# An attention and token-MLP kernel on one core: a fixed order on all engines, hand-numbered PSUM banks, another way for the state and a guarded path with max

## The chip, the cores and the metric

The kernel runs on one core of a Trainium2 chip. The metric is the device time of one execution in microseconds (us), the median of several runs. The core has five engines with queues of their own: TensorE (PE, with its weight loads shown apart as PEld), VectorE (DVE), ScalarE (ACT), GpSimd (POOL) and SyncE (SP). SBUF is the working memory; PSUM, eight banks of 2 KB in each of 128 partitions, takes what TensorE computes, and VectorE and ScalarE copy it out ("evacuate" it).

## What is computed

Cross attention between a sequence `x` (8 batches, 8 heads, 512 tokens, 64 numbers) and a `state` of 32 rows per head, in both directions, and then a token-mixing MLP over the joined result. Cut to what matters:

```python
# x (8, 8, 512, 64), state (8, 8, 32, 64), all float32
scores = scale * x @ state.T;   scores -= scores.max(-1)
a = exp(scores);  a /= a.sum(-1) + 1e-9;     xread = a @ state
scores2 = scale * state @ x.T;  scores2 -= scores2.max(-1)
a2 = exp(scores2); a2 /= a2.sum(-1) + 1e-9;  sread = a2 @ x
y = concat([xread, sread], axis=2)           # heads joined: (8, 544, 512)
wq = y @ w_q;  wk = y @ w_k                  # (8, 544, 64)
mixed = (wq @ wk.T) * scale2 @ y             # (8, 544, 512)
out = maximum(mixed, 0) @ w_out              # (8, 544, 512)
```

## The kernel before

Each batch is one unit of work, and a batch is cut into two halves `u` of its sequence. The steps of a batch are short functions that are called by the names in one list, `ORDER` (line 16). A token such as `pt0.3.t` is the step `pt`, half 0, batch 3, engine `t` (TensorE; `v`, `a`, `p` are VectorE, ScalarE, GpSimd). The list fixes the order of TensorE alone (`manual_schedule`, line 63); the framework orders the other engines from the order of the list and its own rules.

The steps of batch `b`: `ix` (line 141) loads x as bfloat16 through a casting transfer that GpSimd issues; batch 0 comes as four float32 quarters `x_f0` (line 108) and is cast by `xc`. `xT` (line 217) transposes x on TensorE, `xTe` evacuates, `pt` (line 232) computes the scores, `exp` takes their exponential into `E`, without subtracting a maximum. `rs`, `rinv` and `A` (lines 266 to 288) sum and normalise by row; `at`, `ate` (lines 289, 299) transpose `A`. `srd`, `sums` (lines 303, 318) compute the other direction from the same `E`, `srn`, `sbd`, `srT` (lines 330 to 365) normalise it, place it as a block diagonal and transpose it. `wq`, `wk`, `g`, `v` (lines 366 to 462) are the small products of the MLP, `mix` (line 464) with its `relu` the mixed tokens, `fin` (line 509) the product with `w_o`, in pairs of 128 tokens, `oe`, `oc` (lines 521, 527) the copy to `ost` and the transfer to memory. `mixs` and `fs` do the same for the 32 state tokens, four batches at a time.

The state is loaded twice: batch 0 first (line 107), batches 1 to 7 later (line 111), in rows of 256 bytes. `stc` casts it, `stt` (line 173) transposes it, `ste`, `stf` evacuate it into `stT`. The block-diagonal copy `stbd` (128 rows of 4 blocks of 64 columns, zero outside the diagonal), which `v` needs, is filled by four scattering transfers out of `st_bf` (line 166). In `v_mm` all 128 rows take part in each matmul, most of them zeros:

```python
nc.tensor.matmul(out=ps, lhsT=L[b]["wk"][:, NC : NC + 2, :], rhs=L[b]["sbd"], start=True, stop=False)
for r in range(2):
    nc.tensor.matmul(out=ps[:, r, :, :], lhsT=L[b]["g"][:, r, :, :],
                     rhs=stbd[:, b, r, :, :], start=False, stop=(r == 1))
```

PSUM is cut into two pools: `psA` with two buffers of two banks (for `mix`, `fin`, `sw`) and `psB` with four buffers of one bank (all else); a step takes the next free buffer. The output copies of one bank, `ost1`, are used six times (the two `fse` and the four `oc`), and their pool `work` has four buffers (line 79).

Of the kernel before, what the change touches and what calls it, by code (L numbers as in the profile page):

```python
# [8 lines left out]
FP = mybir.dt.float32  # L9
BF = mybir.dt.bfloat16  # L10
# [11 lines left out]
sums.1.t xTe0.2.a A1.0.p pt1.2.t srn.1.v sw.3.t rs1.1.v exp1.2.a sbd.1.p srT.1.t at1.0.t pt0.2.t
rinv.1.v srTe.1.a xT0.3.t rs1.2.v exp0.2.a xT1.3.t A.1.p ate.0.a xTe1.3.v srd.2.t sums.2.t xTe0.3.v
pt1.3.t swe.1.a wq.0.t srn.2.v wks.0.t exp1.3.a rs0.2.v sw.2.t sbd.2.p wqe.0.a srT.2.t wk.0.t
rinv.2.v pt0.3.t srTe.2.a xT1.5.t wke.0.v exp0.3.a A.2.p xT1.4.t swe.3.v g.0.t xTe1.5.a srd.3.t
xTe1.4.v sums.3.t ge.0.a rs0.3.v pt1.5.t pt1.4.t exp1.5.a at.2.t srn.3.v exp1.4.a v.0.t ate.2.v
sbd.3.p srT.3.t swe.2.a at.1.t srTe.3.v rs1.4.v wq.2.t ve.0.a wks.2.t wqe.2.v wk.2.t mix1.0.t
# [24 lines left out]
def kernel(  # L52
# [10 lines left out]
    ctx.enter_context(tc.manual_schedule(engines={mybir.EngineType.PE}))  # L63
# [10 lines left out]
    HN = NP * NS  # L74
    scale = 1.0 / float(D) ** 0.5
# [18 lines left out]
    mask = const.tile([128, NP], BF, name="mask")  # L94
# [3 lines left out]
    rmix = const.tile([128, B, KC, 2, SH], BF, name="rmix")  # L98
# [42 lines left out]
    def load_x(n, b, e):  # L141
        if n == "iwo":
            nc.gpsimd.dma_start(out=w_o, in_=moe_w_out.rearrange("(k p) e -> p k e", p=128))
        else:
            b = int(n[2:])
            nc.gpsimd.dma_start(out=x_bf[b], in_=xsrc(b, 0, H))  # L146

    def x_cast(n, b, e):
        g = int(n[2:])
        o, i = x_bf[0][:, 2 * g : 2 * g + 2], x_f0[:, 2 * g : 2 * g + 2]  # L150
        if e == "p":
            nc.gpsimd.tensor_copy(out=o, in_=i)  # L152
# [9 lines left out]
    def st_cast(n, g, e):
        b0, b1 = (0, 1) if g == 0 else (1, B)
        copy(e, st_bf[:, b0:b1], st_f[:, b0:b1])
        if g == 1:
            for q in range(NP):
                rows = slice(NS * q, NS * q + NS)
                nc.sync.dma_start(
# [419 lines left out]
```

## Time and profile before

| | |
|---|---|
| time, median of three runs | 100.2 us (99.65, 100.2, 100.47) |
| span of the profiled execution, first to last instruction | 98.7 us |
| TensorE busy | 80.1 us in 1288 matmuls |
| ScalarE, VectorE, GpSimd busy | 56.9, 53.3, 35.0 us |
| read from and written to memory | 10.22, 8.91 MB |
| mean granted clock of TensorE | 0.944 of full speed |

The profile gives the span of its execution and no time of its own beside it; the 1.5 us between 98.7 and the median are what lies around the span. Busy time is the time in which an engine runs at least one instruction. Matmuls are pipelined: a group's busy time counts overlap once, the mean of one instruction does not. [...]

### The profile page before, as it was taken

To read this page: it belongs to the slowest core of one execution; us is meant where nothing else is said; L and a number is where in the kernel's file an instruction comes from. 1 tells how busy PE (TensorE), PEld (TensorE's weight loads), DVE (VectorE), ACT (ScalarE), POOL (GpSimd) and SP (SyncE) were. 2 spreads that over 40 slices of the span, in tenths; PEclk is the share of its full clock that TensorE was granted. 3 is DMA by queue.
4 is the path that set the end of the run, shared out by engine and by line. 5 is a ranking of instruction groups with operands and counts; after the bars stand their busy time and mean duration, and the time that the engine had idled before them with its cause. 6 is when DMAs were issued, how large, how long until landed. Compare 5 with 4: busy or idle time off the path is not lost.

```text
span 98.7 us, 2953 instructions
## 1 busy us (share of the span) xinstructions
PE 80.1 (81%) x1288; PEld 53.0 (54%) x1288; DVE 53.3 (54%) x107; ACT 56.9 (58%) x84; POOL 35.0 (35%) x42
## 2 busy tenths in 40 slices
PE   0137699654999999999999979999999999999200
PEld 0025588544889885584655736488646554344000
DVE  5443288870857891899148454555866760423200
ACT  2501958956078588184798776465964733855100
POOL 7289009999084910003800740570035200000000
PEclk9999999996559999999999999999999999999965
DMA  1999999999999200270324650283003255293980
GB/s 45 318 274 147 178 184 216 214 213 201 196 197 166 33 0 0 110 299 23 123 91 176 267 208 11 46 334 145 5 7 130 83 213 206 103 345 54 350 321 10
DMA packets 17044, 15.39 MB, mean 156 GB/s; under 512 B 5768, under 2 KB 14472, under 8 KB 17032
## 3 DMA queue, kind: packets, MB, share of 16 engines
q1 hardware_dynamic: 8392, 9.96, 31.8%
q0 software_dynamic: 7808, 4.19, 31.0%
q10 hardware_dynamic: 832, 1.05, 3.0%
q8 instruction: 10, 0.16, 0.7%
q14 instruction: 2, 0.02, 0.1%
HBM read 10.22 MB, written 8.91 MB: 194 GB/s over the span
## 4 chain that ended last, share of the span: by engine, by line
PE 60%; DMA 26%; POOL 3%; DVE 3%; ACT 2%; issue 1%; SPq 0%; ACTq 0%
PE fin_ps L505 22%; DMA x_bf<-in_x_dram 15%; DMA out_dram<-ost 6%; PE xT_ps L221 5%; PE mix_ps L471 4%; DMA x_f<-in_x_dram 4%; PE at_ps L295 3%; PE pt_ps L237 3%; PE wq_ps L371 3%; PE wk_ps L409 3%; PE srd_ps L308 2%; PE wk_ps L397 2%; PE fins_ps L505 2%; PE g_ps L425 2%; POOL x_bf L146 2%; PE v_ps L440 2%
## 5 line engine op out<-in xcount | busy, mean ns | idle before, releaser
L505 PE MATMUL fin_ps<-w_o,rmix 128*128 128x512 bf16 x128 | 29.9, 379 | 0.0
L282 POOL TENSOR_TENSOR A<-E,rinv 128x1024 bf16<-128x1024 bf16 (+1 forms) x8 | 14.4, 1804 | 21.4 <-DVE rinv L276 11.9
L505 PEld LDWEIGHTS <-rmix 128*128 128x128 bf16 x128 | 11.7, 98 | 12.7 <-issue 0.6
L221 PE MATMUL xT_ps<-ident,x_bf 128*128 128x128 bf16 x128 | 11.9, 255 | 4.1 <-POOL x_bf L152 1.8
L131 ACT COPY ost<-fin_ps 128x1024 f32<-128x1024 f32 (+1 forms) x10 | 9.3, 927 | 10.1 <-PE fin_ps L505 6.1
L137 ACT ACTIVATE rmix<-mix_ps 128x1024 bf16<-128x1024 f32 x12 | 12.2, 1025 | 4.0 <-PE mix_ps L471 4.0
L133 DVE COPY ost<-fin_ps 128x1024 f32<-128x1024 f32 (+1 forms) x8 | 8.7, 1090 | 10.1 <-PE fin_ps L505 10.1
L345 POOL TENSOR_TENSOR sbd<-srn,mask 128x256 bf16<-128x256 bf16 x16 | 9.5, 616 | 12.7 <-DVE srn L335 11.9
L268 DVE TENSOR_REDUCE rsum<-E 128x16 f32<-128x512 bf16 x16 | 10.7, 680 | 5.8 <-ACT E L253 5.7
L221 PEld LDWEIGHTS <-x_bf 128*128 128x128 bf16 x128 | 9.7, 116 | 5.4 <-POOL x_bf L152 2.1
L253 ACT ACTIVATE E<-pt_ps 128x512 bf16<-128x512 f32 x16 | 9.4, 604 | 4.3 <-PE pt_ps L237 3.8
L131 ACT COPY xT<-xT_ps 128x1024 bf16<-128x1024 bf16 x10 | 10.1, 1032 | 1.1 <-PE xT_ps L221 1.1
L237 PE MATMUL pt_ps<-stT,xT 128*128 128x64 bf16 x128 | 6.8, 205 | 0.8 <-ACT xT L131 0.8
L146 POOL DMA_DIRECT2D x_bf<-in_x_dram x7 | 6.8, 975 | 0.0
L237 PEld LDWEIGHTS <-xT 128*128 128x128 bf16 x128 | 5.5, 105 | 2.2 <-ACT xT L131 1.4
L133 DVE COPY xT<-xT_ps 128x1024 bf16<-128x1024 bf16 x6 | 4.1, 688 | 3.7 <-PE xT_ps L221 3.7
L179 PE MATMUL stT_ps<-ident,st_bf 128*64 128x128 bf16 x32 | 2.3, 314 | 4.5 <-DVE st_bf L133 4.5
L471 PE MATMUL mix_ps<-wq,V 64*128 64x256 bf16 x64 | 5.8, 272 | 0.1
L295 PE MATMUL at_ps<-ident,A 128*128 128x128 bf16 x64 | 5.1, 219 | 0.9 <-POOL A L282 0.9
L457 ACT ACTIVATE V<-v_ps 128x512 bf16<-128x512 f32 x6 | 3.6, 598 | 3.4 <-PE v_ps L444 3.2
L139 DVE TENSOR_SCALAR rmix<-mix_ps 128x1024 bf16<-128x1024 f32 x4 | 4.9, 1220 | 0.8 <-PE mix_ps L471 0.8
L295 PEld LDWEIGHTS <-A 128*128 128x128 bf16 x64 | 3.9, 98 | 1.5 <-POOL A L282 1.0
(71 smaller groups left out, 110.4 us busy)
## 6 DMA issues: line engine op xcount, KB each, us to landing
out_dram<-ost SPq DMA_DIRECT2D x14, 512.0 KB, 3.0
x_bf<-in_x_dram POOLq DMA_DIRECT2D x7, 512.0 KB, 12.3
out_dram<-ost SPq DMA_DIRECT2D x4, 256.0 KB, 4.7
x_f<-in_x_dram ACTq DMA_DIRECT2D x2, 256.0 KB, 3.6
x_f<-in_x_dram SPq DMA_DIRECT2D x2, 256.0 KB, 4.0
w_o<-in_moe_w_out_dram POOLq DMA_DIRECT2D x1, 512.0 KB, 12.8
out_dram<-ost ACTq DMA_DIRECT2D x2, 256.0 KB, 4.1
st_f<-in_state_dram SPq DMA_DIRECT2D x1, 448.0 KB, 6.4
```

Of the source, the lines that this page charges most:

```text
L131: nc.scalar.copy(out=out, in_=in_)
L133: nc.vector.tensor_copy(out=out, in_=in_)
L137: nc.scalar.activation(out=out, in_=in_, func=AF.Relu)
L221: nc.tensor.transpose(out=ps[:, h, :], in_=x_bf[b][:, h, 128 * u : 128 * u + 128], identity=ident)
L237: nc.tensor.matmul(out=ps[:, :, r, NS * q : NS * q + NS], lhsT=L[b][f"xTe{u}"][:, h, :], rhs=stT[:, b, h, :, :], start=(h == 0), stop=(h = ...
L253: nc.scalar.activation(out=L[b]["E"][:, 2 * u : 2 * u + 2].rearrange("p c r q n -> p c r (q n)"), in_=L[b][f"pt{u}"], func=AF.Exp, scale=f ...
L268: nc.vector.reduce_sum(out=L[b]["rsum"][:, w], in_=L[b]["E"].rearrange("p c r q n -> p (c r q) n")[:, w], axis=AX.X,)
L282: eng.tensor_tensor(out=L[b]["A"].rearrange("p c r q n -> p (c r q) n")[:, w], in0=L[b]["E"].rearrange("p c r q n -> p (c r q) n")[:, w], ...
L295: nc.tensor.transpose(out=L[b]["at"][:, r, c, :], in_=L[b]["A"][:, c, r, :, :], identity=ident)
L345: nc.gpsimd.tensor_tensor(out=L[b]["sbd"][:, r], in0=L[b]["srn"][:, r : r + 1, :].to_broadcast((128, NP, D)), in1=mask[:, :, None].to_broa ...
L471: nc.tensor.matmul(out=ps[:, h, kk, :], lhsT=L[b]["V"][rows, 128 * k : 128 * k + 128], rhs=L[b]["wq"][rows, 0:SH], start=True, stop=True,)
L505: nc.tensor.matmul(out=ps, lhsT=lhs(k), rhs=w_o[:, k, :], start=(k == 0), stop=(k == KC - 1))
```

## The change

- All engines follow the list now, not TensorE alone. A token has five parts: step, index, batch, engine, PSUM bank. The output transfers are tokens of their own (`d`, `dc`, `ds`), on SP.
- PSUM is one tile of eight banks, and each step is told its bank.
- The state is loaded once, as 128 rows of 4 KB (`st_c`), cast in halves, and transposed in 32 transposes. The block diagonal comes from `stT` by 64 small transposes (`sp`) and two products with a mask for each half of the batches (`stbd`); it has two blocks for each half of 64 rows in place of four for 128, and `v` works in two halves of 64 rows that write different banks.
- x0 and x1 come as float32 in plain quarter loads and are cast by engines. GpSimd's casting loads of x2 to x7 are spread over the list, the one of `w_o` comes after batch 0's `A`.
- Four groups of dummy matmuls (`dm`, 23, 17, 8 and 7 of 128 columns) stand at the start of TensorE's order.
- `A` and the reciprocals always go in halves.
- Output copies have a pool of their own with six buffers.
- The sums are kept in `chk`. At the end `ok` tests that all lie between 2^-60 and 2^60, `okm` and `oke` count them, every engine reads the count, and if it falls short a second program, `with_max`, computes all batches again with the maximum subtracted.

The core of the diff:

```diff
 ORDER = """
...
+xc.0.2.a.0 xc.0.0.p.0 xc.0.3.p.0 xc.0.1.v.0 ix.0.2.p.0 dm.128.23.t.7 xp.1.0.t.0 xp.0.0.t.1
+dm.128.17.t.7 xp.0.2.t.1 stc.0.1.p.0 xp.1.2.t.0 xp.1.3.t.0 xp.0.1.t.1 stc.0.0.v.0 xp.1.1.t.0
+xTe.1.0.a.0 xp.0.3.t.1 dm.128.8.t.7 stt.0.0.t.2 xc.1.2.p.0 dm.128.7.t.7 stt.0.1.t.2 xc.1.0.v.0
+xTe.0.0.v.0 ste.0.0.a.0 xq.1.0.t.0 ste.0.1.a.0 xc.1.1.v.0 stf.1.0.v.0 xq.1.2.t.0 xc.1.3.p.0
+xq.0.0.t.1 xq.1.1.t.0 wc.0.0.p.0 pt.0.0.t.4 xq.1.3.t.0 xq.0.2.t.1 xq.0.3.t.1 pt.1.0.t.5
+stf.1.1.a.0 ste.0.2.v.0 xq.0.1.t.1 xTe.1.1.v.0 xTe.0.1.v.0 exp.0.0.a.0 exp.1.0.a.0 sp.0.0.t.6
+stf.1.2.a.0 srd.0.0.t.7 pt.0.1.t.0 pt.1.1.t.1 rs.1.0.v.0 sums.0.0.t.7 sw.0.3.t.4 rs.0.0.v.0
+exp.1.1.a.0 rv.0.0.v.0 rs.1.1.v.0 swe.0.3.a.0 sp.0.1.t.6 rv.1.0.v.0 exp.0.1.a.0 sw.0.0.t.2
+A.0.0.p.0 srn.0.0.v.0 sw.0.1.t.4 rv.1.1.v.0 A.1.0.p.0 srd.0.1.t.0 rs.0.1.v.0 ix.0.3.p.0
...
+fin.3.2.t.0 at.0.3.t.5 d.0.1.s.0 exp.0.4.a.0 exp.1.4.a.0 xT.0.5.t.4 ix.0.6.p.0 xTe.1.5.v.0
+oe.1.1.a.0 at.1.3.t.5 pt.1.5.t.6 rs.0.4.v.0 srT.0.3.t.7 rs.1.4.v.0 sbd.0.3.v.0 xTe.0.5.a.0
+fin.0.2.t.2 exp.1.5.a.0 rv.0.4.v.0 ate.0.3.v.0 srTe.0.3.v.0 pt.0.5.t.4 wks.0.3.t.5 rs.1.5.v.0
+wq.0.3.t.6 exp.0.5.a.0 A.0.4.p.0 srd.0.4.t.7 srd.0.5.t.4 rv.1.4.v.0 oe.1.2.v.0 sums.0.4.t.7
+wqe.0.3.a.0 wk.0.3.t.5 wke.0.3.a.0 A.1.4.p.0 fin.1.2.t.2 sums.0.5.t.4 srn.0.4.v.0 d.1.1.s.0
+at.1.4.t.5 rs.0.5.v.0 oe.0.2.a.0 ix.0.7.p.0 srT.0.4.t.0 g.0.3.t.1 srn.0.5.v.0 xT.0.6.t.6
...
+mse.0.7.v.0 d.1.4.s.0 fs.0.7.t.6 fin.0.6.t.2 fin.1.6.t.2 mxe.0.7.v.0 fin.2.7.1.7 fse.0.7.v.0
+fin.3.7.1.6 fin.1.7.1.4 fin.0.7.1.5 oe.0.4.a.0 d.0.4.s.0 oe.0.6.a.0 oc.2.7.v.0 ds.0.7.s.0
+oc.1.7.v.0 okm.0.0.t.7 oc.3.7.a.0 d.0.6.s.0 dc.3.7.s.0 oc.0.7.a.0 dc.2.7.s.0 dc.1.7.s.0 dc.0.7.s.0
+oke.0.0.v.0
...
-    ctx.enter_context(tc.manual_schedule(engines={mybir.EngineType.PE}))
+    ctx.enter_context(tc.manual_schedule())
...
-    psA = ctx.enter_context(tc.tile_pool(name="psA", bufs=2, space=bass.MemoryType.PSUM))
-    psB = ctx.enter_context(tc.tile_pool(name="psB", bufs=4, space=bass.MemoryType.PSUM))
+    ostp = ctx.enter_context(tc.tile_pool(name="ostp", bufs=6))
+    gen = ctx.enter_context(tc.tile_pool(name="gen", bufs=1))
+    psum = ctx.enter_context(tc.tile_pool(name="psum", bufs=1, space=bass.MemoryType.PSUM))
...
+    banks = psum.tile([128, 8, 512], FP, name="banks")
+    def one(k):
+        return banks[:, k, :]
+    def two(k):
+        return banks[:, k : k + 2, :]
...
-    nc.sync.dma_start(out=st_f[:, 0], in_=st_src[:, 0:2])
+    st_cs = state.rearrange("b h (g j) d -> (b h g) j d", j=16)
     for g in range(4):
-        eng = nc.sync if g % 2 == 0 else nc.scalar
-        eng.dma_start(out=x_f0[:, 2 * g : 2 * g + 2], in_=xsrc(0, 2 * g, 2 * g + 2))
-    nc.sync.dma_start(out=st_f[:, 1:B], in_=st_src[:, 2 : 2 * B])
+        eng = nc.sync if g % 2 else nc.scalar
+        eng.dma_start(out=x_f[0][:, 2 * g : 2 * g + 2], in_=xsrc(0, 2 * g, 2 * g + 2))
+    nc.sync.dma_start(out=st_c, in_=st_cs)
+    for g in range(4):
+        nc.sync.dma_start(out=x_f[1][:, 2 * g : 2 * g + 2], in_=xsrc(1, 2 * g, 2 * g + 2))
...
+    def dummy(i, b, e, k):
+        for _ in range(b):
+            nc.tensor.matmul(out=one(k)[:, 0:i], lhsT=fill[:, 0:128], rhs=fill[:, 0:i], start=True, stop=True)
...
+    def st_sp(i, g, e, k):
...
+        for b in range(4 * g, 4 * g + 4):
+            for r in range(2):
+                for q in range(NP):
+                    nc.tensor.transpose(
+                        out=G["sp"][NS * q : NS * q + NS, b, r, :],
+                        in_=stT[0:64, b, NP * r + q, 0, :],
+                        identity=ident[0:64, 0:64],
+                    )
+    def st_bd(i, g, e, k):
+        for q in range(2):
+            out = stbd[:, 4 * g : 4 * g + 4, :, q, :]
+            in_ = G["sp"][:, 4 * g : 4 * g + 4]
+            if e == "a":
+                nc.scalar.activation(out=out, in_=in_, func=AF.Copy, scale=mask[:, q : q + 1])
+            else:
+                nc.vector.tensor_scalar(
+                    out=out, in0=in_, scalar1=mask[:, q : q + 1], scalar2=None, op0=ALU.mult
+                )
...
+    def v_mm(i, b, e, k):
+        ps = two(k)[:, :, 0 : 4 * D].rearrange("p m (r t) -> p m r t", r=2)
+        for m in range(2):
+            rows = slice(64 * m, 64 * m + 64)
+            nc.tensor.matmul(
+                out=ps[:, m],
+                lhsT=L[b]["wk"][rows, NC : NC + 2, :],
+                rhs=L[b]["sbd"][rows],
+                start=True,
+                stop=False,
+            )
         for r in range(2):
+            for m in range(2):
+                rows = slice(64 * m, 64 * m + 64)
+                nc.tensor.matmul(
+                    out=ps[:, m, r, :],
+                    lhsT=L[b]["g"][rows, r, :, :],
+                    rhs=stbd[rows, b, r, :, :],
+                    start=False,
+                    stop=(r == 1),
+                )
...
+    def ok_v(i, b, e, k):
+        nc.vector.tensor_scalar(out=okay, in0=chk, scalar1=1.0 / LIM, scalar2=None, op0=ALU.is_ge)
+        nc.vector.scalar_tensor_tensor(
+            out=okay_bf, in0=chk, scalar=LIM, in1=okay, op0=ALU.is_le, op1=ALU.mult
+        )
+    def ok_mm(i, b, e, k):
+        G["ok"] = one(k)[0:1, 0 : B * (NR + 2)]
+        nc.tensor.matmul(
+            out=G["ok"], lhsT=ones, rhs=okay_bf.rearrange("p b j -> p (b j)"), start=True, stop=True
+        )
+    def ok_ev(i, b, e, k):
+        nc.vector.reduce_sum(out=n_ok, in_=G["ok"], axis=AX.X)
+        nc.vector.tensor_copy(out=n_ok_i, in_=n_ok)
...
+    good = nc.values_load(n_ok_i[0:1, 0:1])
+    with tc.If(good < 128 * B * (NR + 2), preferred_fallthrough_block=False):
+        ident_f = gen.tile([128, 128], FP, name="ident_f")
+        nc.vector.tensor_copy(out=ident_f, in_=ident)
+        for b in range(B):
+            with_max(b)
```

## Rows read from the trace of the kernel before

**Rows 1.** The page, part 1: busy time, share of span, instructions.

```profile
PE 80.1 (81%) x1288; PEld 53.0 (54%) x1288; DVE 53.3 (54%) x107; ACT 56.9 (58%) x84; POOL 35.0 (35%) x42
```

**Rows 2.** Busy time by stretch: from:to, length, each engine, clock, DMA share, GB/s.

```profile
12.56:16.00 3.44, 3.44 (x98) 3.14 (x96) 2.76 (x6) 2.11 (x3) 0.97 (x3) 1.00 1.45 196
16.00:23.69 7.69, 4.39 (x140) 3.41 (x123) 5.13 (x13) 6.32 (x10) 7.67 (x10) 0.94 1.63 213
23.69:29.40 5.71, 5.71 (x117) 4.89 (x118) 3.38 (x8) 1.81 (x5) 2.96 (x3) 0.50 1.45 195
29.40:91.98 62.58, 61.73 (x909) 37.94 (x906) 37.23 (x68) 41.00 (x60) 16.44 (x17) 1.00 0.38 129
91.98:98.70 6.72, 0.01 (x1) 0.00 (x0) 0.00 (x0) 0.58 (x1) 0.00 (x0) 0.68 0.58 221
...
12.56:23.69 11.13, 7.83 (x212) 6.55 (x211) 7.89 (x18) 8.43 (x13) 8.64 (x12) 0.96 1.58 208
```

**Rows 3.** The same view for line 221, x's transposes (PE, PEld, clock).

```profile
12.90:15.00 2.10, 1.90 (x16) 1.68 (x16) 1.00 1.46 192
...
23.60:25.70 2.10, 1.89 (x16) 1.63 (x16) 0.50 1.44 192
29.40:30.60 1.20, 1.14 (x16) 0.98 (x16) 0.92 1.46 207
```

**Rows 4.** Timeline of the start: start, length, instruction, idle time before it.

```profile
11.03 0.61 PE L237 MATMUL pt_ps<-stT,xT 128*128 128x64 bf16 x8 [0.78 <-ACT xT L131]
...
15.93 2.62 POOL L146 DMA_DIRECT2D x_bf<-in_x_dram  x3
...
20.64 1.06 POOL L282 TENSOR_TENSOR A<-E,rinv 128x512 bf16<-128x512 bf16 x1
...
21.76 0.40 PE L295 MATMUL at_ps<-ident,A 128*128 128x128 bf16 x4 [0.90 <-POOL A L282]
```

**Rows 5.** The chain of work that ended last: start, length, what.

```profile
8.53 15.12 DMA x_bf<-in_x_dram
...
34.54 0.33 PE mix_ps L471 x4
...
37.44 1.73 PE fin_ps L505 x8
...
55.66 0.35 PE srd_ps L308 x32
...
69.27 0.22 PE v_ps L440
69.49 0.22 PE v_ps L444 x2
69.70 0.54 PE mix_ps L471 x8
...
87.13 6.08 DMA out_dram<-ost
```

**Rows 6.** Timeline of the end, ScalarE and its queue.

```profile
93.31 0.58 ACT L131 COPY ost<-fin_ps 128x512 f32<-128x512 f32 x1 [2.42 <-DMA out_dram<-ost]
93.92 0.36 ACTq L531 DMA_DIRECT2D out_dram<-ost  x1
```

**Rows 7.** Groups by line and form: busy us, mean ns, idle time before.

```profile
L133 DVE CAST wq<-wq_ps 128x288 bf16<-128x288 f32 x4 | 1.8, 457 | 1.5 <-PE wq_ps L380 1.5
...
L282 POOL TENSOR_TENSOR A<-E,rinv 128x512 bf16<-128x512 bf16 x1 | 1.1, 1064 | 0.0
```

**Rows 8.** The tile x_bf: its transfers, from issue to landing.

```profile
DMA to landing us min/median/max: 6.9/12.3/15.1
```

**Rows 9.** The page, part 6: transfers by queue, KB each, us to landing.

```profile
x_f<-in_x_dram SPq DMA_DIRECT2D x2, 256.0 KB, 4.0
...
st_f<-in_state_dram SPq DMA_DIRECT2D x1, 448.0 KB, 6.4
```

**Rows 10.** The page, part 3: the queue of instruction fetches: packets, MB, share.

```profile
q8 instruction: 10, 0.16, 0.7%
```

More of the change, by code (lines that the diff above doesn't have):

```diff
@@ L22 @@
[L22 to L27, printed above, removed]
@@ L156, in w_cast @@
-    def w_cast(n, b, e):
-        nc.gpsimd.tensor_copy(out=w_qk[:, :, 0:2, :], in_=w_f)
-        nc.gpsimd.tensor_copy(out=w_qk[:, :, 2, :], in_=w_f[:, :, 1, :])
-    SG = [(0, 1), (1, 4), (4, B)]
[L162 to L168, printed above, removed]
-                    out=stbd[rows, :, :, q, :].rearrange("p b r d -> p (b r) d"),
-                    in_=st_bf[rows].rearrange("p b r d -> p (b r) d"),
-                )
@@ new lines, in st_bd, with st_tr @@
+    def st_bd(i, g, e, k):
[7 more added lines that the diff above has]
+                    out=out, in0=in_, scalar1=mask[:, q : q + 1], scalar2=None, op0=ALU.mult
+                )
+    def st_tr(i, g, e, k):
+        if "st" not in G:
+            G["st"] = two(k).rearrange("p k m -> p (k m)").bitcast(BF).rearrange(
+                "p (j m) -> p j m", j=16
+            )
+        for j in range(8 * g, 8 * g + 8):
+            for c2 in range(2):
+                nc.tensor.transpose(
+                    out=G["st"][64 * c2 : 64 * c2 + 64, j, :], in_=st_cb[:, j, :], identity=ident
+                )
@@ new lines, in st_ev @@
+    def st_ev(half, g, e, k):
+        b0, b1 = SG[g]
+        for c2 in range(2):
+            rows = slice(64 * c2, 64 * c2 + 64)
+            copy(
+                e,
+                stT[rows, b0:b1, :, c2, :].rearrange("p b h (g j) -> p (b h) g j", g=2)[
+                    :, :, :, 8 * half : 8 * half + 8
+                ],
+                G["st"][rows, 8 * half : 8 * half + 8, 16 * b0 : 16 * b1].rearrange(
+                    "p j (m g) -> p m g j", g=2
+                ),
+            )
@@ L198, in sw_mm @@
+    def sw_mm(i, p, e, k):
+        ps = two(k)
         for bb in range(2):
@@ L533, in fs_mm, with fin_ev @@
-    def fs_mm(n, b, e):
-        ps = psB.tile([128, DM], FP, name="fins_ps", tag="psB")
-        fin_acc(ps, lambda k: rmix_s[:, b // 4, k].rearrange("p b n -> p (b n)"))
-        L[b]["fs"] = ps
-    def fs_ev(n, b, e):
-        ost = work.tile([128, DM], FP, name="ost1")
-        copy(e, ost, L[b]["fs"])
-        j = b // 4
-        nc.sync.dma_start(out=out[4 * j : 4 * j + 4, S:SP, :], in_=ost)
+        fin_acc(ps, lambda j: L[b]["rmix"][:, j, c // 2, t0 : t0 + 128])
+    def fin_ev(p, b, e, k):
+        L[b]["o", p] = ostp.tile([128, 2, DM], FP, name="ost")
+        copy(e, L[b]["o", p], L[b]["fin", p])
@@ new lines, in fin_st, with fin_ev1, fin_st1, fs_mm @@
+    def fin_st(p, b, e, k):
+        nc.sync.dma_start(out=dst_x[b, :, 2 * p : 2 * p + 2, :], in_=L[b]["o", p])
+    def fin_ev1(c, b, e, k):
+        L[b]["o1", c] = ostp.tile([128, DM], FP, name="ost1")
+        copy(e, L[b]["o1", c], L[b]["fin1", c])
+    def fin_st1(c, b, e, k):
+        (nc.scalar if e == "a" else nc.sync).dma_start(out=dst_x[b, :, c, :], in_=L[b]["o1", c])
+    def fs_mm(i, b, e, k):
+        L[b]["fs"] = one(k)
+        fin_acc(L[b]["fs"], lambda j: rmix_s[:, b // 4, j].rearrange("p b n -> p (b n)"))
@@ new lines, in fs_ev, with fs_st @@
+    def fs_ev(i, b, e, k):
+        L[b]["os"] = ostp.tile([128, DM], FP, name="ost1")
+        copy(e, L[b]["os"], L[b]["fs"])
+    def fs_st(i, b, e, k):
+        for t in range(4):
+            nc.sync.dma_start(
+                out=out[b - 3 + t, S:SP], in_=L[b]["os"][NS * t : NS * t + NS]
+            )
+    def ok_v(i, b, e, k):
+        nc.vector.tensor_scalar(out=okay, in0=chk, scalar1=1.0 / LIM, scalar2=None, op0=ALU.is_ge)
+        nc.vector.scalar_tensor_tensor(
+            out=okay_bf, in0=chk, scalar=LIM, in1=okay, op0=ALU.is_le, op1=ALU.mult
+        )
```

466 lines of the change are left out of this document (272 added, 194 removed).

## The prediction

> **What bounds the kernel now.** I read the page's busy times first: TensorE (PE) is busy for 80.1 of 98.7 us, no other engine for 60 [rows 1]. So the end is PE's work plus the time in which PE stands still or runs slowly. The table by stretch of time shows where that is [rows 2]. From 29.40 to 91.98 us PE is busy for 61.73 of 62.58 us at full clock: nothing is to be had there but less work. The losses are elsewhere. [...]
>
> Why PE starves from 16 to 23.69 us (4.39 busy of 7.69) stands in the timeline: GpSimd (POOL) issues three casting x loads in a row, 2.62 us, then `sbd`, then a fourth load, and only at 20.64 us the second half of batch 0's normalised scores `A`, for which PE's transposes wait until 21.76 [rows 4]. Then PE waits for batch 3, whose load took 15.12 us [rows 5]. The clock falls in this starved stretch. In the tail the last output copy waits 2.42 us for an older output transfer, which took 6.08 us: the pool's `ost1` has four buffers, and six copies use it [rows 5, 6].
>
> **The change part by part.** *Start.* State comes in one load of 128 rows of 4 KB, in place of a first small one and one of 448 KB that took 6.4 us; a 256 KB quarter of x in the same plain form took 4.0 us [rows 9], so I estimate some 4 to 6 us for it. x1 comes in four such quarters behind it on SP's queue. Ahead of `pt.0.0` PE now has 16 transposes of x0, 32 of state, 8 of x1, and 55 dummy matmuls of 128 columns; 32 of these dummies stand between the real ones. [...] `pt.0.0` began at 11.03 us [rows 4]; I expect it at 11 to 14. Against that lateness stands that batch 1 is transposed by then, 1.1 to 1.9 us of work. I put the two against each other: 0, with bounds of 1.5 us gained and 2 lost.
>
> *From 12.56 to 23.69.* Two batches, not one and a half, are there, and POOL's order is `A.0.0`, `A.1.0`, then the load of x3; a half of `A` costs 1.06 us on POOL [rows 7]. That removes the 2.62 us and the 0.9 us of issuing from in front of `A`. How dense PE gets lies between the old 7.83 of 11.13 (0.70) and the 0.99 of the steady part; ScalarE and VectorE have to evacuate for two batches at once here, so I take the middle, 0.85: idle time falls from 3.30 to 1.67, a gain of 1.6 (bounds 0 and 3.2). If the dummies have raised the clock before 12.56, the 3.44 us up to 16.00 become 3.44 x 1.14 / 1.90 = 2.06: gain 1.4 (bounds 0 and 1.4).
>
> *23.69 to 29.40.* Without the starvation ahead of it the clock should stay up: 5.71 / 2 = 2.85 gained (bounds 0 and 2.85).
>
> *`sp`, `stbd`.* The block-diagonal state is made by 64 transposes with 32 output rows and 64 columns in place of four scattered transfers. The nearest row is `srd`, 32 matmuls of that shape in 0.35 us, so 0.7 us; as full transposes they would cost 64 x 0.07 = 4.5. They are like `srd`: I take 1.0, on PE's path. The two mask products on each of ScalarE and VectorE go beside PE.
>
> *`v`.* 1024 columns per batch over 128 rows, 0.22 + 0.22 us, become the same columns in two row halves, each writing its own bank. `mix` runs so: four matmuls of 256 columns take 0.33 us, eight take 0.54 [rows 5], so four, the columns of one `v`, cost 0.33. Gain 8 x 0.11 = 0.9 (bounds 0 and 8 x 0.17 = 1.4).
>
> *Other engines.* VectorE gets four more halves of `A`, six pairs of `sbd`, a `stbd` pair and the split reciprocals, some 24 small instructions; at 0.46 us each (a 288-element evacuation [rows 7]) that is 11 us on top of 53.3. POOL loses about ten. Neither reaches PE. SP issues all output transfers behind separate tokens, as before in the order of the copies. This costs nothing as long as PE, at some 73 us of full-clock work, is the longest.
>
> *Middle.* The x loads of batches 4 to 7 are no longer early but spread. The fastest load took 6.9 us [rows 8]. Between the token of x6's load and its first transpose PE has 5.3 us of work (two `fin` at 1.73 / 2 each [rows 5], and fourteen short groups at prices like those beside it); so a load that starts only where its token stands comes 1.6 us late, and four of them 6.4 us. POOL has little to do and will mostly be there earlier, which makes 0 the other bound. With what a new fixed order may cost beside, I take 1.5 lost, nearer to 0 because the old order left only 0.85 us idle in 62.58.
>
> *Tail.* `ostp` has six buffers. The wait before the last copy goes: the copy could start at about 92.0 in place of 93.31 [rows 2, 6], 1.3 gained (bounds 1.0 and 1.4). The transfer behind it stays.
>
> *Guard.* After the last matmul come one small matmul, a reduction of 272 numbers (at most 0.46 [rows 7]) and a conversion, then each engine reads a number and branches around the path with max. The last output transfer, issued at 93.92 of 98.7 us, covers some 4 us of this [rows 6]; so 0 is the lower bound. [...] I take 0.5, as the transfer covers most.
>
> [...]
>
> **Sum.** 98.7 - 1.6 - 1.4 - 2.85 + 1.0 - 0.9 + 1.5 - 1.3 + 0.5 = 93.65 us of span. The median of the runs is 100.2 against a span of 98.7; with the same 1.5 us around it: 95.1, so 95.0.
>
> **Rivals.** *1, slower: waits on the one PSUM buffer.* Eight banks in one tile with bank numbers by hand: where a bank is named again before its evacuation, or a wait is kept for more than the bank, PE stops for an evacuation, 0.5 to 1.2 us. For it speaks that 0.85 us of idle time leaves much to lose and that the four buffers of one bank rotated freely before; against it that there are still eight banks. From some ten such waits of 0.9 us in the steady part the gain is gone, and at fifteen the time is about 95 + 13 = 108. *2, late loads:* the middle loses 4 to 6 us, time 97.5 to 99.5, about 98. For it: 5.3 against 6.9 us; against it: POOL's free time. [...] *4, the start does nothing:* the dummies and x1 hold up `pt.0.0`, ScalarE and VectorE limit the first two batches, the clock falls again; the 5.85 us of the first three terms are missing, time 100.9. For it: `pt.0.0` isn't earlier; against it: the chain behind `A` gets plainly shorter.
>
> **How the numbers follow.** Forecast 0.58 (91.5 to 97), rival 1 0.11, rival 2 0.14, rival 3 0.08, rival 4 0.09. A measurement of this kernel can tell about 1%, so faster is below 99.2: the forecast, nearly all of rival 2 and most of rival 3, 0.77; within 1%: the rest of these and about half of rival 4, 0.08; slower: rival 1 and the rest of rival 4, 0.15. The range leaves out rival 1 and rival 4 and reaches down to where middle and guard cost nothing: 91.5 to 99.5.
>
> **What would show it.** Right: full clock from the first batch on, `pt.0.0` at 11 to 14 us, the second half of batch 0's `A` before 18, first `fin` before 30 us (37.4 before [rows 5]), `v` at about 0.33 us, last copy straight behind the last matmul, no idle time between the last landing and the end. Wrong: PE waiting for x4 to x7 (rival 2), for copies out of PSUM (rival 1), a clock of 0.50 after 16 us or `pt.0.0` after 15 us (rival 4), several us of waits behind the last transfer (rival 3).

## The result, and the profile after

The changed kernel takes 95.12 us (median of 94.94, 95.31, 93.73 and 95.36), the kernel before beside it 99.98 us. The ratio is 0.944, with a 95% interval of 0.936 to 0.952. The forecast was 95.0 us. That it was hit is partly luck, as the traces below show: the guard came out 2.7 us worse than its term, the tail 1.2 us better, and 2 us of gain stood in no term. Some runs of a kernel are over 1.5% longer than its fastest; ratios leave them out, medians do not.

| | before | after |
|---|---|---|
| profiled execution: time, span (us) | 99.65, 98.7 | 94.94, 93.1 |
| last output matmul ends (us) | 91.98 | 85.66 |
| from there to the end (us) | 6.72 | 7.4 |
| TensorE busy (us) | 80.1 | 78.3, of it 5.8 in dummies |

So TensorE (PE) is done 6.3 us sooner, and 0.7 us of that is given back behind it. The page of after, parts 1 and 2 (busy time; granted clock in 40 slices, in tenths of full speed) and the dummies from part 5, against [rows 1]:

```profile
PE 78.3 (84%) x1424; PEld 54.9 (59%) x1432; DVE 57.9 (62%) x136; ACT 57.8 (62%) x94; POOL 25.5 (27%) x34
...
PEclk9999999958999999999999999999999999999985
...
L195 PE MATMUL banks<-fill 128*128 128x128 bf16 x55 | 5.8, 288 | 1.0 <-DVE warm L165 1.0
```

PE is still the busiest engine. VectorE and ScalarE rose to 57.9 and 57.8 us, GpSimd fell by 9.5. The clock row still has a dip, in slices 9 and 10. The table by stretch, of after, in the columns of [rows 2]; the DMA share there is the busy time of sixteen transfer engines, and one queue alone had more than 1 of it (of the 1.45 from 23.69 to 29.40 us in the kernel before, 1.44 is GpSimd's q0):

```profile
12.56:16.00 3.44, 2.28 (x104) 1.95 (x102) 3.37 (x7) 2.64 (x5) 0.34 (x1) 1.00 0.35 53
16.00:23.69 7.69, 6.83 (x210) 5.56 (x209) 5.47 (x17) 6.00 (x12) 5.96 (x8) 0.78 0.55 67
23.69:29.40 5.71, 5.52 (x158) 4.76 (x153) 4.98 (x13) 4.94 (x11) 3.13 (x3) 1.00 0.73 106
...
29.40:85.66 56.26, 54.12 (x846) 34.26 (x848) 37.99 (x82) 37.87 (x57) 10.16 (x10) 1.00 0.69 180
...
85.70:89.00 3.30, 0.17 (x1) 0.00 (x0) 0.57 (x2) 0.58 (x1) 0.00 (x0) 1.00 0.87 313
89.00:93.10 4.10, 0.00 (x0) 0.00 (x0) 0.00 (x0) 0.00 (x0) 0.00 (x0) 0.63 0.04 10
```

From 23.69 to 29.40 the clock is 1.00 in place of 0.50; from 29.40 on PE is idle for 2.14 us, 0.85 before [rows 2]. After the last matmul the data are out by 89.0 us, and then 4.1 us pass in which next to nothing moves. The same view in single microseconds places the dip:

```profile
18.00:19.00 1.00, 0.92 (x45) 0.79 (x34) 1.00 (x2) 1.00 (x3) 1.00 (x2) 0.70 0.00 0
19.00:20.00 1.00, 1.00 (x23) 0.61 (x22) 1.00 (x4) 0.04 (x1) 0.52 (x1) 0.50 0.00 0
20.00:21.00 1.00, 1.00 (x18) 0.81 (x12) 0.45 (x3) 0.99 (x2) 0.71 (x1) 0.50 0.81 65
21.00:22.00 1.00, 1.00 (x16) 0.83 (x16) 0.69 (x1) 1.00 (x2) 1.00 (x2) 0.60 0.89 100
```

Estimated as one minus the granted clock in each of these microseconds, it costs 0.3 + 0.5 + 0.5 + 0.4 = 1.7 us of PE work. The timeline of PE (start, length, instruction, idle time before it), against [rows 4]:

```profile
11.92 0.40 PE L309 MATMUL banks<-stT,xT 128*128 128x64 bf16 x8
...
13.14 0.41 PE L221 MATMUL banks<-ident,stT 64*32 64x64 bf16 x32
...
16.33 0.31 PE L268 MATMUL banks<-w_qk,stT 64*32 64x128 bf16 x16 [1.43 <-POOL w_qk L183]
16.44 0.48 PE L221 MATMUL banks<-ident,stT 64*32 64x64 bf16 x32
...
30.80 1.03 PE L583 MATMUL banks<-w_o,rmix 128*128 128x512 bf16 x3
```

The first scores come at 11.92 us (11.03 before), the 64 `sp` transposes take 0.41 + 0.48 us, and the first `fin` comes at 30.80 in place of 37.44 us [rows 5]. The chain that ended last shows what sets the pace between 16 and 27.5 us, and one wait later on:

```profile
16.71 0.58 ACT sw L181
17.30 0.51 ACT E L323
17.83 0.69 DVE chk L332
18.52 0.67 DVE A L345
19.18 0.80 DVE stbd L234 x2
20.00 1.26 ACT stbd L232 x2
21.27 0.90 ACT AT L181
...
26.05 1.37 POOL A L345
...
47.71 9.89 DMA x_bf<-in_x_dram
57.65 1.07 PE banks L288 x16
```

Before, this stretch of the chain was a load of 15.12 us and then PE [rows 5]; now it is ScalarE, VectorE and GpSimd. So a dip of the clock there should cost little, as PE isn't the last to finish; the run with x1's casting load below bears that out (no dip, and the first `fin` at 30.80 us as here). The end of the kernel, as a timeline, and line 753 (the branch), whose columns are times of one: shortest, median, longest in ns, first and last start:

```profile
85.59 0.28 PE L632 MATMUL banks<-okay_bf,ones 128*1 128x272 bf16 x1
85.70 0.58 ACT L181 COPY ost<-banks 128x512 f32<-128x512 f32 x1 [1.14 <-PE banks L583]
85.91 0.43 DVE L637 TENSOR_REDUCE n_ok<-banks 1x1 f32<-1x272 f32 x1 [0.38 <-PE banks L632]
86.37 0.14 DVE L638 CAST n_ok_i<-n_ok 1x1 int32<-1x1 f32 x1
```

```profile
L753 PEldq COMPARE_BRANCH  x2: 95/1972/3850, 87.6 to 87.9; - x2
L753 DVEq COMPARE_BRANCH  x2: 51/53/55, 87.6 to 87.8; - x2
L753 SPq COMPARE_BRANCH  x2: 38/44/49, 87.6 to 89.0; - x2
```

The last copy (85.70) stands directly behind the last matmul, without the 2.42 us of [rows 6]. In this trace each branch of the other four engines takes 0.04 to 0.055 us and PE's shorter one 0.10, but PE's jump around `with_max` takes 3.85 us, from 87.9 to about 91.75. SP, which waits for the output transfers first, is done at 89.0.

### The profile page after: what moved, and what is told of

It is laid out like the page before. It is cut to its first block, busy times and chain, and to the rows that moved or that the text cites. A ratio compares the mean times of both kernels' runs of the same rounds, so it can differ in the third digit from the quotient of the medians.

```text
span 93.1 us, 3320 instructions
## 1 busy us (share of the span) xinstructions
PE 78.3 (84%) x1424; PEld 54.9 (59%) x1432; DVE 57.9 (62%) x136; ACT 57.8 (62%) x94; POOL 25.5 (27%) x34
## 4 chain that ended last, share of the span: by engine, by line
PE 48%; DMA 25%; ACT 7%; DVE 6%; POOL 3%; issue 2%; SPq 1%; POOLq 0%
PE banks L583 28%; DMA x_bf<-in_x_dram 11%; DMA w_f<-in_moe_w_k_dram 8%; DMA st_c<-in_state_dram 7%; PE banks L288 4%; PE banks L548 4%; DVE chk L332 3%; POOL A L345 3%; ACT E L323 2%; PE banks L357 2%; PE banks L309 2%; ACT stbd L232 1%; PE banks L442 1%; PE banks L496 1%; ACT sw L181 1%
## 5 line engine op out<-in xcount | busy, mean ns | idle before, releaser
L583 PE MATMUL banks<-w_o,rmix 128*128 128x512 bf16 x121 | 29.3, 379 | 0.5 <-issue 0.2
L345 POOL TENSOR_TENSOR A<-E,rinv 128x512 bf16<-128x512 bf16 x11 | 12.3, 1122 | 29.1 <-DVE rinv L340 21.4
L181 ACT COPY ost<-banks 128x1024 f32<-128x1024 f32 (+1 forms) x15 | 13.9, 929 | 7.3 <-PE banks L583 7.2
L288 PE MATMUL banks<-ident,x_bf 128*128 128x128 bf16 x128 | 10.8, 235 | 3.4 <-POOL x_bf L183 2.2
L332 DVE TENSOR_REDUCE chk<-E 128x16 f32<-128x512 bf16 x16 | 10.6, 680 | 3.0 <-ACT E L323 2.9
L189 ACT ACTIVATE rmix<-banks 128x1024 bf16<-128x1024 f32 x10 | 10.1, 1033 | 2.3 <-PE banks L548 1.5
L323 ACT ACTIVATE E<-banks 128x512 bf16<-128x512 f32 x16 | 9.5, 601 | 3.1 <-PE banks L309 2.7
L185 DVE COPY xT<-banks 128x1024 bf16<-128x1024 bf16 x11 | 7.4, 683 | 5.6 <-PE banks L288 5.5
L191 DVE TENSOR_SCALAR rmix<-banks 128x1024 bf16<-128x1024 f32 x6 | 7.3, 1218 | 0.8 <-PE banks L548 0.6
L357 PE MATMUL banks<-ident,A 128*128 128x128 bf16 x64 | 6.3, 230 | 0.7 <-POOL A L345 0.6
```

Source lines behind the costliest of these rows:

```text
L189: nc.scalar.activation(out=out, in_=in_, func=AF.Relu)
L288: nc.tensor.transpose(out=L[b]["xT", u][:, h, :], in_=x_bf[b][:, h, 128 * u : 128 * u + 128], identity=ident,)
L323: nc.scalar.activation(out=L[b]["E"][:, 2 * u : 2 * u + 2].rearrange("p c r q n -> p c r (q n)"), in_=L[b]["pt", u], func=AF.Exp, scale=fl ...
L332: nc.vector.reduce_sum(out=chk[:, b, w], in_=L[b]["E"].rearrange("p c r q n -> p (c r q) n")[:, w], axis=AX.X,)
L345: eng.tensor_tensor(out=L[b]["A"].rearrange("p c r q n -> p (c r q) n")[:, w], in0=L[b]["E"].rearrange("p c r q n -> p (c r q) n")[:, w], ...
L357: nc.tensor.transpose(out=L[b]["at"][:, r, c, :], in_=L[b]["A"][:, c, r, :, :], identity=ident)
```

## The experiments

The first three runs and the one with the count earlier are from one chip, the others from two more, on which the changed kernel itself was not run. Each stands beside the kernel before on its own chip, so they are compared by their ratios to it.

**The changed kernel again**, as the measure for the others.

> The changed kernel unaltered, as the level for the other runs beside it: 95 us, ratio to the kernel before 0.94 to 0.955.

95.06 us, ratio 0.9435 [0.9363, 0.9507]; PE's jump took 3.87 us. The dip of the clock is longer in this profile, and its span is 92.9 us, not longer:

```profile
16.00:23.69 7.69, 6.96 (x167) 5.64 (x156) 5.97 (x18) 5.78 (x12) 5.37 (x6) 0.56 0.58 69
```

**Without the guard.**

```diff
-... ok.0.0.v.0 ... okm.0.0.t.7 ... oke.0.0.v.0
-    good = nc.values_load(n_ok_i[0:1, 0:1])
-    with tc.If(good < 128 * B * (NR + 2), preferred_fallthrough_block=False): ...
```

> The test of the sums, its count, the branch and the path with max are left out; all else is the changed kernel. Theory (the guard is not covered by the last transfer: PE's branch over the other path takes 3.85 us in the profile and everyone waits for it): 2 to 3 us less than the unaltered one, so 92 to 93 us, and the program ends within 1.5 us of the last landing. Rival (the guard is hidden behind the last transfer, as the prediction's 0.5 us had it; the long tail comes from the transfer): at most 0.7 us less.

92.52 us, 0.9223 [0.917, 0.9275]: the guard costs 2.5 us by the medians, 2.1% by the ratios.

**The branch kept, the path behind it cut to one copy.**

```diff
-        for b in range(B):
-            with_max(b)
```

> The path with max is left out except for one copy, so that the branch jumps over next to nothing; test, count, reading and branch stay. Theory (the price of the guard is the fetch of code behind the jump): PE's branch falls from 3.85 to about 0.1 us and the time falls nearly to that of the kernel without a guard, at most 0.8 us above it. Rival (the price is reading the number and meeting): PE's jump is short, but the time stays within 0.7 us of the unaltered one.

92.9 us, 0.9306 [0.9258, 0.9355]. Counting, reading the number and branching are all still there and cost 0.4 of the 2.5 us (0.8 of the 2.1% by the ratios), which is within the uncertainty. The rest goes with PE's jump, as line 753 of this kernel shows:

```profile
L753 PEldq COMPARE_BRANCH  x2: 86/133/180, 87.5 to 87.6; - x2
```

0.18 us in place of 3.85. Its last output matmul ends at 85.55 us, the span is 89.8: a tail of 4.25 us. The page's part 3 (a queue of instruction fetches: packets, MB, share), first of the changed kernel, then of this one:

```profile
q8 instruction: 13, 0.21, 1.0%
```

```profile
q8 instruction: 11, 0.18, 0.8%
```

The other queue of instructions, q14, has 7 packets against 2. Between 87.9 and 91.75 us, while PE jumps, one packet of q8 and four of q14 run (0.02 and 0.03 MB); behind the branch of this run there is none. So code is fetched during the long jump.

**The path cut to one batch of eight**, on another chip (the kernel before: 100.0 us).

```diff
-        for b in range(B):
+        for b in range(1):
```

> The changed kernel with the guarded path cut to one batch of eight (left out: the other seven batches of the path that this data never takes). PE then jumps over about 290 instructions and not 2250. Theory: the jump's time goes with fetching what lies behind it, in steps: over 290 instructions it is 0.2 to 1 us in place of 3.85, and the time is that of the kernel without the guarded body, 92.5 to 93.5. Rival: any jump out of what has been fetched costs the same; PE's jump still takes over 3 us and the time stays at 94.5 to 95.5.

95.83 us, 0.9579 [0.9534, 0.9624]. The theory fell, the rival holds: over an eighth of the instructions the jump costs the same, and one packet of q8 and two of q14 run in it. The time is 0.3 us above the rival's range.

```profile
L753 PEldq COMPARE_BRANCH  x2: 91/1950/3810, 88.5 to 88.8; - x2
```

**The count earlier.**

```diff
-... mixs.0.6.t.3 mxe.0.4.a.0 v.0.7.t.0 mse.0.6.v.0 ... okm.0.0.t.7 ... oke.0.0.v.0
+... mixs.0.6.t.3 okm.0.0.t.7 mxe.0.4.a.0 v.0.7.t.0 mse.0.6.v.0 oke.0.0.v.0 ...
```

> Only the count of the good sums is moved ahead, to the seventh batch's MLP, so that the number is there when TensorE ends; the branch stays where it is. Theory (PE's jump of 3.85 us starts late because it waits for reduction, conversion and reading of the number, 1.9 us behind the last matmul): the jump starts about 1.5 us sooner and the time falls by 1 to 1.8 us against the unaltered one. Rival (the branch waits for the output transfers, not for the number): no change, within 0.4 us.

95.82 us, 0.9513 [0.9441, 0.9584]: no gain. (At this place the count's product goes into bank 7 while half a `mix` of batch 4 is still there, so that part of the output isn't computed; I read the time alone.) The jump starts 3 us sooner, as the theory had it, and nothing is gained: PE now jumps at 84.9 us, directly behind its work, but beside the last output transfers, and both get longer: the jump to 4.87 us, the slowest of the last transfers from 2.7 to 4.8 us.

```profile
L753 PEldq COMPARE_BRANCH  x2: 91/2480/4870, 81.9 to 84.9; - x2
```

**Six buffers for the output copies, in the kernel before.**

```diff
+    ostp = ctx.enter_context(tc.tile_pool(name="ostp", bufs=6))
-        ost = work.tile([128, DM], FP, name="ost1")      # twice
+        ost = ostp.tile([128, DM], FP, name="ost1")
```

> The kernel before with one edit: six buffers for the one-bank output copies in place of four. Theory (the prediction's term for the tail): the last copy no longer waits 2.42 us, it starts straight behind the last matmul, and the time falls by 1.0 to 1.4 us against the kernel before, ratio 0.986 to 0.990. Rival (the transfers share the engines, the last landing comes no sooner): ratio 0.995 to 1.

100.08 us, 1.0019 [0.9995, 1.0043]: nothing, though the wait is gone. The timeline of its end:

```profile
91.35 0.58 ACT L132 COPY ost<-fin_ps 128x512 f32<-128x512 f32 x1 [1.14 <-PE fin_ps L506]
91.97 0.36 ACTq L532 DMA_DIRECT2D out_dram<-ost  x1
```

The copy starts at 91.35 and not at 93.31 [rows 6], the last transfer is issued 1.95 us sooner (0.67 of it because PE ends sooner in this profile, at 91.31), and the span is 98.2, 6.2 us after that issue (4.8 before). Where the time goes, the stretches around the last matmul show, in the columns of [rows 2]: first the kernel before, then this one, then the changed one.

```profile
88.00:91.98 3.98, 3.98 (x19) 1.61 (x17) 1.38 (x2) 1.60 (x2) 0.00 (x0) 1.00 0.47 127
```

```profile
88.00:91.31 3.31, 3.26 (x15) 1.27 (x14) 1.38 (x2) 1.50 (x2) 0.00 (x0) 1.00 0.41 94
91.31:98.20 6.89, 0.01 (x1) 0.00 (x0) 0.00 (x0) 0.58 (x1) 0.00 (x0) 0.77 0.57 219
```

```profile
82.00:85.70 3.70, 3.65 (x17) 1.55 (x16) 1.38 (x2) 1.60 (x2) 0.00 (x0) 1.00 0.90 322
```

Before, the transfers stand half idle in the last 4 us of PE's work (a share of 0.47, 127 GB/s), and 6.72 us x 221 GB/s = 1.5 MB still move after it [rows 2]. With six buffers it is 6.89 x 219, again 1.5 MB. In the changed kernel 322 GB/s flow while PE still works, and 3.30 x 313 GB/s = 1.0 MB are left. Behind the last matmul the transfers are full at first: a share of 1.00 to 1.01 and 379 to 393 GB/s from 92 to 95 us in the kernel before, 363 to 393 from 91 to 95 with six buffers. So I read the tail as set by how much is still to be written when PE ends, which a buffer for one copy doesn't change. No run altered that amount alone.

**Without the dummies** (the four `dm` tokens are dropped).

```diff
-... dm.128.23.t.7 ... dm.128.17.t.7 ... dm.128.8.t.7 ... dm.128.7.t.7
```

> The changed kernel without the 55 dummy matmuls. Theory (the dummies raise TensorE's clock before the first state transposes and otherwise fill waits): the transposes at 7 to 11 us take twice as long, the granted clock rises only at about 15 us, and the time is 1 to 2.5 us above the unaltered changed kernel (95.06), 96 to 97.5. Rival (the dummies stand in the way, the real transposes raise the clock soon enough): equal or up to 1 us faster.

94.38 us (92.91 to 96.56), 0.9324 [0.9287, 0.9361]. The dummies bring nothing; without them the kernel is as fast or a little faster. PE's longest wait at the start, for x0's cast, becomes 4.9 us, which is where the dummies had stood, and the clock stays at 1.00 from 12.56 to 29.40 us. The 32 transposes of the state do take longer, 1.85 us in place of 1.14, as the theory had it; the time doesn't follow.

**w_q and w_k from ScalarE's queue** (the chain of after has a load of w_k from 8.29 to 15.52 us).

```diff
-            nc.sync.dma_start(out=w_f[64 * r : 64 * r + 64, :, t, :], in_=wsrc[t][r])
+            nc.scalar.dma_start(out=w_f[64 * r : 64 * r + 64, :, t, :], in_=wsrc[t][r])
```

> In the changed kernel w_q and w_k are loaded from ScalarE's queue in place of SP's, where they stood behind state and x1 and landed at 15.5 us. Theory (TensorE's idle 1.43 us at 14.9 to 16.3 us waits for these weights, and with what follows lets the clock fall to 0.50 from 18.6 to 21.6 us): the weights land by 11 us, the gap goes, the clock doesn't fall, and the time is 1.5 to 3 us lower, 92 to 93.5. Rival (x1 and state come later by as much, as all share the transfer engines): within 0.7 us of 95.06.

96.89 us, 0.9684 [0.9646, 0.9723]: slower by 1.8 us by the medians, 2.5% by the ratios, which neither side expected. PE's wait of 1.43 us for the weights is gone and the clock stays at 1.00 from 12.56 to 29.40 us, as the theory had it, but the first `fin` comes at 32.98 us in place of 30.80. ScalarE's timeline:

```profile
1.80 1.45 ACTq L162 DMA_DIRECT2D w_f<-in_moe_w_q_dram  x2
4.34 2.05 ACTq L162 DMA_DIRECT2D w_f<-in_moe_w_k_dram  x2
...
7.82 0.60 ACT L181 CAST x_bf<-x_f 128x512 bf16<-128x512 f32 x1
```

The issues themselves hold ScalarE until 6.4 us; its cast of x0 slips from 5.86 to 7.82 us, and the first scores from 11.92 to 14.34.

**x1 by a casting load of GpSimd, as before** (the four plain loads and the four `xc.1` tokens are dropped, `ix.0.1.p.0` stands ahead of `ix.0.2.p.0`).

> In the changed kernel batch 1 comes by GpSimd's casting load again, ahead of batch 2's, in place of four plain quarters and four casts. Theory (two batches early is what keeps TensorE busy from 12.5 us on): batch 1 lands 1 to 3 us later, TensorE idles in front of its transposes, time 0.7 to 2.5 us above 95.06. Rival (the form of x1's load is indifferent, half the bytes into SBUF even help): within 0.5 us or faster.

94.8 us, 0.9485 [0.945, 0.952]: no difference. PE does wait, 1.92 us, for batch 1, whose transposes come at 12.66 us; but later it catches up:

```profile
16.00:23.69 7.69, 5.53 (x210) 4.48 (x192) 6.64 (x19) 6.30 (x13) 5.38 (x6) 1.00 0.53 69
```

This run has no dip of the clock: PE is busy for 5.53 us with 210 matmuls, in the changed kernel for 6.83 us with as many. It gains nothing by it: at 22.2 us it stands still for 1.1 us until ScalarE has copied `AT`, and from there on its groups start at the same times as in the changed kernel, `wk` at 22.22 (22.23), `fin` at 30.80 (30.80).

**The state in rows of 256 bytes; then the block diagonal by scattering transfers too** (same chip as the one-batch run). In the first, the state's casts and evacuations follow the other layout.

```diff
-    nc.sync.dma_start(out=st_c, in_=st_cs)
+    nc.sync.dma_start(out=st_c.rearrange("p b r d -> p (b r) d"), in_=st_src)
```

> The changed kernel with the state loaded in its old form, rows of 256 bytes, in one transfer; the 4 KB rows and their strided evacuations are gone, all else stays. Theory: the load comes up to 2 us later or at the same time (state was never what the first scores waited for last), and the time stays within 1% of the changed kernel, 94 to 96. Rival: the 4 KB rows are what lets the first scores start at 11.9 us; with 256-byte rows they start 2 us or more later and the time is 96.5 to 98.

95.58 us, 0.9547 [0.9486, 0.9608]. Batch 0's scores come at 11.96 us, those of batch 1 1.6 us later than in the changed kernel, and the 4 KB rows are worth at most about 1%, and nothing against the one-batch run beside it (95.83 us, the changed kernel but for its guarded path). The clock is 1.00 from 16.00 to 23.69 us here, with the dummies in place, and the span is 92.8 us, as with the longest dip.

```diff
-... sp.0.0.t.6 ... sp.0.1.t.6 ... stbd.0.1.v.0 ... stbd.0.0.a.0
+                nc.sync.dma_start(out=stbd[rows, :, :, q % 2, :]..., in_=st_cb[rows]...)   # 4 times
```

> The kernel of the run with 256-byte rows and beside it the block diagonal in its old way: four scattering transfers from the cast state on SP's queue, no sp transposes and no mask products. Theory (the sum has 1.0 us on PE's path for sp): against the run with 256-byte rows PE has 0.9 us less to do, so 0.5 to 1 us faster, unless the scatter is late for the first v, which comes only at about 30 us. Rival: the four scatters, many small pieces, sit ahead of x1's or the weights' transfers and of the x loads on the engines that move data, and the time is 1 us or more longer.

97.55 us, 0.9624 [0.9579, 0.9668]: 0.8% above the run with 256-byte rows by the ratios, whose intervals overlap, and 2.0 us by the medians, most of it from the two longest of four runs. So the theory's gain isn't there, and a loss isn't shown clear of noise. PE has 0.9 us less to do, but waits 1.3 us for x, which it didn't do in the run with 256-byte rows; the x loads themselves take no longer (8.0 us as a median, 8.5 there), the scatters 5.6.

**In the kernel before, four x loads behind A** (`ix4`, `ix5` after `A1.0`, `ix6`, `ix7` after `A.1`).

```diff
-... ix4.0.p ... ix5.0.p ... ix6.0.p ... ix7.0.p
+... A1.0.p ix4.0.p ix5.0.p ... A.1.p ix6.0.p ix7.0.p
```

> The kernel before with one thing of the change: GpSimd issues the loads of x4 and x5 behind batch 0's second half of A, those of x6 and x7 behind batch 1's A, in place of ahead of them. Theory (the second term of the prediction's sum): issuing keeps A from PE; the second half of A comes about 2 to 3.5 us sooner, PE is denser from 16 to 23.7 us, and the time falls by 1 to 3 us, to 97 to 99. Rival: the loads of x2 and x3 bound this stretch anyway; A comes sooner, PE then waits for x3 as before, and the time stays within 1% of the kernel before (99 to 101), with the clock at 0.50 from 23.7 to 29.4 as before.

101.21 us, 1.0098 [1.0028, 1.0168]: slower by 1%. Its timeline of GpSimd and PE:

```profile
18.14 1.04 POOL L282 TENSOR_TENSOR A<-E,rinv 128x512 bf16<-128x512 bf16 x1
...
22.94 1.89 PE L221 MATMUL xT_ps<-ident,x_bf 128*128 128x128 bf16 x16 [1.36 <-ACT E L253]
...
29.43 1.07 PE L221 MATMUL xT_ps<-ident,x_bf 128*128 128x128 bf16 x16 [0.58 <-DMA x_bf<-in_x_dram]
```

`A` comes 2.5 us sooner, as meant, but PE's next transposes then wait for the exponential and come only 0.75 us sooner, still with 1.89 us at half clock; and PE waits 0.58 us for a load at 29.43. The transfers stay as busy as they were: a share of 1.54 and 1.40 from 16.00 and from 23.69 us on, 1.63 and 1.45 before [rows 2], against 0.55 and 0.73 in the changed kernel. So this run moves GpSimd's issues, but does not thin out the loads as the change does.

## Why the prediction was right, and where only its sum was

*The front, forecast -1.6 - 1.4 - 2.85.* In PE's own work the signs were right. PE's idle time from 12.56 to 23.69 us fell from 3.30 to 2.02 us, 1.3 gained for 1.6. The 1.4, for a first stretch at half clock in the kernel before, is a term that no run shows: the record has a clock of 1.00 there [rows 2]. What points to it is that sixteen transposes took 1.90 us at 12.90 and 1.14 at 29.40 us [rows 3]; and where the dummies were left out the 32 transposes of the state took 1.85 us for 1.14, but the time did not rise. In the trace of after no half-clock record lies before 18 us. From 23.69 to 29.40 PE does 5.52 us of work at full clock against an estimated 5.71 x 0.50 = 2.86, 2.7 for 2.85. What the forecast did not have is the dip from 18 to 22 us, 1.7 us of PE work lost again. "Full clock from the first batch on" was wrong, and the first `fin` came at 30.80 and not before 30.

That the lower clock cost the kernel before 2.85 us of time is not shown, and the record speaks against it. With six buffers its clock was 0.73 in place of 0.50 over that stretch:

```profile
23.69:29.40 5.71, 4.83 (x121) 4.06 (x119) 4.37 (x9) 2.36 (x5) 3.77 (x4) 0.73 1.45 198
```

PE then waited 0.88 us for a load of x, its next transposes came at 28.82 in place of 29.41 us, and the time was the same. And 5.71 us at 0.50 take 0.029 from the mean clock: 15 runs of the kernel before with a mean of 0.98 or more, which have no room for it, took 99.5 to 100.4 us, seven with less than 0.95 took 99.8 to 100.4 (three more, at 0.934 and 0.935, took 101.3 to 102.3). So the lost work is real and its price was luck: as far as this shows, something else, most likely the loads with their share of 1.45, set the pace there.

The cause that I gave for the starvation, GpSimd's issues in front of `A`, is not sufficient either: `A` ahead of four of the issues, taken alone, brought nothing. That fewer loads at a time free the front is the rival that fits, and no run tests it. Nor is any one part of the new start the cause: the dummies, x1's plain loads and the 4 KB rows can each go without a loss of more than about 1%. What is left is the new order with its spread loads as a whole; which of its moves are needed wasn't separated. Rival 4's sign, a clock of 0.50 after 16 us, appeared without its price: with a clock of 0.56 or 0.78 from 16 to 23.69 us the spans of the changed kernel are 92.9 and 93.1, the run with x1's casting load has the same first `fin` at 1.00, and of the four runs of the result the one with the lowest mean clock, 0.940, has the shortest span, 91.8, the one with the highest, 0.978, the longest, 93.6.

*`sp`, forecast +1.0:* 0.41 + 0.48 = 0.9 us, 0.64 if each is taken to the start of the next group (the forecast's 0.07 us for a full transpose is 1.14 / 16 [rows 3]). *`v`, forecast 0.33 a batch:* the timeline of after has a single `v` at 29.77 with the next work at 30.09 (0.32), and three in a row that start at 64.84 and give way at 65.61, 0.26 each:

```profile
29.77 0.28 PE L513 MATMUL banks<-sbd,wk 64*128 64x256 bf16 x2
29.89 0.28 PE L523 MATMUL banks<-stbd,G 64*128 64x128 bf16 x4
30.09 0.64 PE L309 MATMUL banks<-stT,xT 128*128 128x64 bf16 x16
...
64.84 0.28 PE L513 MATMUL banks<-sbd,wk 64*128 64x256 bf16 x2
...
65.61 0.41 PE L468 MATMUL banks<-w_qk,srT 128*64 128x128 bf16 x8
```

*The middle, forecast +1.5:* idle time from 29.40 on rose by 2.14 - 0.85 = 1.3 us, 1.2 of it one wait, for x7, whose load took 9.89 us. Rival 2's mechanism was there, at one load and not at four.

*What the sum left out.* PE ended 6.3 us sooner; the terms above, as measured, do not reach that. From 29.40 us on it has 7.6 us less work (54.12 for 61.73) and 1.3 us more idle time. From the starts of PE's groups after 29.40 us (from one group to the next, idle time taken off) I worked out a split: about 3.4 us is work already done by then, which is what the front brought, `sp` taken off (forecast 4.85); 1.2 us is `v`; and about 2 us is that other small products follow each other faster, `mixs`, `mix` and `wks` by 0.4 to 0.5 us each. The 24 `g` of three batches in one group are not part of it: 0.24 us a batch, where one batch took 0.23 to 0.32 us before. The remaining 0.9 us falls on `fin`, of whose 136 matmuls the trace of after holds 128, and can't be read. I had put "a new fixed order" on the side of the costs only. No run separates this gain; it is read from the trace, not shown.

*The tail, forecast -1.3, and the guard, +0.5: both terms failed.* The tail without a guarded path is 4.25 us against 6.72, a gain of about 2.5 and not 1.3, and not for the reason I gave: six buffers alone brought nothing. The error was to price a wait of ScalarE as if the end hung on it, when, as the stretches read, the end hung on 1.5 MB still to be written. The guard cost 2.5 us by the medians, 2.1% by the ratios, 7.4 - 4.25 = 3.2 in the tails of two profiles. That is the side of rival 3, which had 0.08: several us of waits behind the last transfer. The step that failed is "the transfer covers most": the last four transfers land 2.3 to 2.7 us after their issue, not some 4, they cover SP's part only, and PE's jump starts after the count and outlasts the landings by some 2.7 us. No run shows the guard's 0.5, and the sum has no term for this jump; the kernel before, with ten instruction packets [rows 10], has no such branch to read one from. On PE it took 3.85 us with five instruction packets in it over the whole path, 0.18 us and none over one copy; the other four engines jump over their part of the path in 0.04 to 0.055 us. In the profiles the errors nearly cancel: PE's end 2.0 us better than the sum had it (6.3 for 4.25), the tail 1.2 better, the guard 2.7 worse, together 0.5, as 93.1 stands to 93.65.

## What to carry to other kernels

Here a guard at the end was paid by the engine with the longest jump (PE's 3.85 us), though the path behind it is never taken; shortening that path to an eighth didn't help (3.81 us), so judge it by the jump in the trace and not by its length. As I read these tails, a wait there is worth something only if the data behind it could have left sooner (a wait of 2.42 us went with six buffers, and the ratio was 1.0019): add up what is still to be written when the last product ends. A stretch at the lower clock did not cost the work that is lost in it (5.71 us at 0.73 in place of 0.50 left the kernel before at the same time), as I read it because loads or other engines set the pace: ask what PE would wait for at full clock. And test a start-up trick by leaving it out: here 55 dummy products at the start changed nothing for the better.

## What the runs showed of the hardware that I had not expected

PE's jump over the guarded path took 3.81 to 3.87 us whether one batch's instructions or those of eight lay under it, 0.18 us when next to none did, and 4.87 us beside output transfers; the other engines branch in 0.04 to 0.055 us. Why PE differs stays open (the path also holds fewer instructions for the others: by the code some 30 of VectorE's a batch, about 290 of PE's), and a layout in which the usual way needs no jump wasn't tried. Issuing transfers held ScalarE: two issues of 0.60 us each spanned 2.05 us of its queue, and its cast of x0 came at 7.82 in place of 5.86 us. And the clock's dip to 0.50 behind 16 us came in some runs of nearly the same program and not in others (0.56, 0.78, 1.00 over one stretch). From 16.40 to 18.40 us, just ahead of the fall, PE was busy for 1.54 us in the changed kernel; in the run with 256-byte rows, where the clock didn't fall, it was 0.96. What decides it stays open.
